# Regrouping the tail, a packed head and casting transfers in an attention and feed-forward kernel

## The chip, the cores and the metric

The kernel runs on one core of a Trainium2 chip. The metric is device time of one launch in microseconds, lower is better. Five engines work side by side and are tied by semaphores: PE (TensorE, the matmuls; its weight loads stand apart as PEld), DVE (VectorE), ACT (ScalarE), POOL (GpSimd) and SP (SyncE, which mostly issues transfers). Transfers between HBM and the core's SBUF are carried out by 16 DMA engines.

## The reference

Linear attention with decay over 4 batches, 8 heads, 768 tokens and head dimension 64, then a bilinear feed-forward with 512 inputs and 1536 inner columns. All inputs and the output are float32. The attention goes block by block and carries a 64 x 64 state for each batch and head:

```python
for b in range(nb):
    qb, kb, vb = (q[:, :, sl], k[:, :, sl], v[:, :, sl])
    intra = einsum('bhic,bhjc->bhij', qb, kb) * Dmask
    intra = einsum('bhij,bhjd->bhid', intra, vb)
    inter = einsum('bhid,bhde->bhie', qb * lam_pow, kv_state)
    out[:, :, sl] = intra + inter
    kv_state = lam_block * kv_state + einsum('bhsd,bhse->bhde', kb * rev_pow, vb)
x = out.transpose(0, 2, 1, 3).reshape(3072, 512)
return ((x @ w_a) * (x @ w_b)) @ w_out
```

## The kernel before

**Units and groups.** The 3072 tokens are 24 units of 128 tokens, six to a batch, each with all 8 heads. GROUPS cuts the units into groups, g0 to g7, of 4, 1, 2, 4, 4, 4, 4 and 1 units. A group's attention is written transposed into a tile xT (four slices s of 128 features by up to 512 tokens), and then its feed-forward runs while the attention of the next group's units is woven in.

**Attention of a unit.** q and k are multiplied by powers of lambda and cast to bf16 (scale, L401, called by make_ks and make_qs), v is cast (make_vb, L418 and L420). q and k are transposed, by PE (piece_T) for units 4 to 6 and by a transposing transfer of SP (in prep_k) from unit 7 on. scores (kq, L457) are 8 matmuls, two to a head pair; mask (L480) multiplies them by the triangle lotri; intra and inter (o_mm, L497) build o_ps, which evac_o copies to xT (L520). kv_update and kv_copy keep the state.

**The head.** Units 0 to 3 are the first group, and nothing can be hidden under a feed-forward yet. Their q and k are loaded with 4 tokens to a partition, so that rows are 1 KB long (x4), scaled (scale4, L877), transposed (transpose4, L886), and put back in natural order of tokens by the copies of unpack (L897). natural_k transposes k once more. v is loaded in natural order. scores4 (L922) and the functions above do the rest; warm issues idle matmuls.

**Weights.** w_a and w_b come in six chunks of 256 columns each, w_out in six of 256 rows, all as f32 by SP's queue into staging tiles (load_w, tile wst), and are cast to bf16 by DVE, ACT or POOL (cast_w, L240 to L254) while g0 runs. A list, pending, holds the order of all loads; pump issues the next as soon as a staging slot is free or, for q, k and v, the unit is no more than LOOKAHEAD ahead.

**Feed-forward.** Plain groups (g0, g1, g2, g7) take for each of the 12 blocks f of 128 inner columns four matmuls for a (a_ps) and four for b (b_ps, both L596); ACT copies a (L605), DVE multiplies (L623), and the product is multiplied by w_out (op, L643). Groups 3 to 6 (Z_GROUPS) make a and b by seven half-size products in place of eight (ffn_z, tiles U, V, W, L730): the halves of xT are added and subtracted first (x_sums, L705 to L707), so are the quarters of the weights (weight_sum, L267 to L275), and ACT and DVE put the products together in a tile oab (L736, L767 to L769), whose halves DVE multiplies into ab (L738). Groups 4 to 6 (ZO_GROUPS) make the multiplication by w_out by seven products too, in 14 halves H (out_half, L852), which are woven into the next group's feed-forward; they need sums of ab (ab_sum, SM in the plan) and of w_out (out_sum, WO). The last group is one plain unit, between whose matmuls the halves H of g6 stand; its output leaves in three pieces, of 256, 128 and 128 columns.

**Order.** PLAN is a table written by hand: for each group, at which slot of the feed-forward which piece (T, S, V, O, P, C, H, ...) is issued. Each engine works through its own instructions in the order in which they are issued. The tables VB_ENG, KV_ENG, SUM_ENG, XS_ENG and the like choose the engine of a piece.

Of the kernel before, what the change touches and what calls it, by code (L numbers as in the profile page):

```python
# [22 lines left out]
def _bc(ap, dims):  # L23
# [8 lines left out]
LOOKAHEAD = {9: 2, 10: 1}  # L32
DMA_T = range(7, 24)
KEEP_GROUPS = 2
PACK = 4

PLAN = {
# [38 lines left out]
}  # L81
Z_GROUPS = (3, 4, 5, 6)
ZO_GROUPS = (4, 5, 6)
FIN_AT = 5
N_LATE = 3
EV_ENG = {(u, b): "act" for u in range(24) for b in range(2)}
MASK_ACT = dict(enumerate([0] * 7 +
                        [1] +
                        [0] * 3 +
                        [1] * 2 +  # L90
                        [0] * 4 +
                        [1] * 3 +
                        [0] +
                        [1] +
                        [0] * 2))
KV_ENG = dict(enumerate(["dve"] * 10 + ["act"] * 2 + ["dve"] + ["act"] * 11))
VB_ENG = dict(enumerate(["pool"] * 7 +
                        ["dve"] * 3 +
                        ["pool"] * 5 +
                        ["dve"] * 2 +  # L100
                        ["act"] +
                        ["pool"] +
                        ["dve"] +
                        ["pool"] +
                        ["act"] * 3))
SUM_ENG = {(3, 0): 'dve', (3, 1): 'dve', (3, 2): 'pool', (3, 3): 'dve', (3, 4): 'pool', (3, 5): 'pool', (3, 6): 'dve', (3, 7): 'dve', (4, 0): 'dve', (4, 1): 'pool', (4, 2): 'pool', (4, 3): 'pool', (4, 4): 'dve', (4, 5): 'pool', (4, 6): 'pool', (4, 7): 'pool', (5, 0): 'dve', (5, 1): 'dve', (5, 2): 'pool', (5, 3): 'pool', (5, 4): 'dve', (5, 5): 'pool', (5, 6): 'pool', (5, 7): 'dve', (6, 0): 'pool', (6, 1): 'dve', (6, 2): 'pool', (6, 3): 'dve', (6, 4): 'dve', (6, 5): 'pool', (6, 6): 'dve', (6, 7): 'dve'}
XS_ENG = {(3, 0): 'dve', (3, 1): 'dve', (3, 2): 'dve', (4, 0): 'dve', (4, 1): 'dve', (4, 2): 'dve', (5, 0): 'dve', (5, 1): 'pool', (5, 2): 'pool', (6, 0): 'pool', (6, 1): 'pool', (6, 2): 'pool'}
WS_ENG = {0: 'dve', 1: 'dve', 2: 'dve', 3: 'dve', 4: 'dve', 5: 'dve', 6: 'dve', 7: 'pool'}
WO_ENG = {0: 'dve', 1: 'dve', 2: 'pool', 3: 'dve', 4: 'dve'}
CO_ENG = {0: 'pool', 1: 'pool', 2: 'pool', 3: 'dve', 4: 'dve', 5: 'dve'}  # L110
# [3 lines left out]
def kernel(  # L114
# [40 lines left out]
    raw_pool = ctx.enter_context(tc.tile_pool(name="raw", bufs=1))  # L155
# [16 lines left out]
    def z_bank(name, i):  # L172
        return ps_pool.tile([128, 2, 256], F32, name=name, tag=f"ps{i}")
# [5 lines left out]
    raw = {}  # L179

    def load_x(w, u):
        b, nb = divmod(u, NB)
        if w == "v" and u == GROUPS[0] - 1:
            t = o_pool.tile([128, H, D], F32, name="vf", tag="osb")
        else:
            t = ld_pool.tile([128, H, D], F32, name=w + "f", tag=w + "f")
        nc.sync.dma_start(out=t, in_={"q": qr, "k": kr, "v": vr}[w][b, nb])
        raw[u, w] = t
# [7 lines left out]
    staged = {}  # L196
    HN, NP = d_model // 2, FC // 2

    def sum_tile(shape, dt, name, tag):
        return sum_pool.tile(shape, dt, name=name, tag=tag)  # L200

    ab_stage = ab_pool.tile([128, 3, 1024], F32, name="wst", tag="ab")
    slots = [lambda: oab_pool.tile([128, 1024], F32, name="wst", tag="oab")] * 2
    slots += [lambda i=i: ab_stage[:, i] for i in range(3)]
    slots += [lambda t=t: sum_tile([128, 1024], F32, "wst", t) for t in ("zab", "wy0", "wy1")]
    once = lambda: xT_pool.tile([128, 1024], F32, name="wst", tag="xT")
    slots.insert(0, once)
# [8 lines left out]
    def load_w(kind, c):  # L216
        slot = slots.pop(0)
        t = slot()
        if kind == "o":
            t = t.rearrange("p (k n) -> p k n", k=2)  # L220
            nc.sync.dma_start(out=t, in_=wo_r[:, 2 * c:2 * c + 2, :])
        else:
            w = W_CHUNKS[c]
            t = t[:, :KS * w].rearrange("p (k n) -> p k n", k=KS)
            r = wa_r if kind == "a" else wb_r
            if c in W_HALVES:
                t = t.rearrange("p k n -> p (k n)").rearrange("p (k n) -> p k n", k=2)
            nc.sync.dma_start(out=t, in_=w_part(r, c))
        staged[kind, c] = t, slot

    def cast_w(kind, c, eng):
        t, slot = staged.pop((kind, c))
        if slot is not once:
            slots.append(slot)
        if kind == "o":
            dst = wo_sb[:, 2 * c:2 * c + 2, :]
        else:
            dst = w_part(wa_sb if kind == "a" else wb_sb, c)
        if eng == "act":
            nc.scalar.copy(dst, t)  # L240
        elif eng == "pool":
            nc.gpsimd.tensor_copy(dst, t)
# [50 lines left out]
    for cs in W_STEPS:  # L293
        pending += [("a", c) for c in cs] + [("b", c) for c in cs]
# [784 lines left out]
```

## Time and profile before

| | |
|---|---|
| median of 3 runs | 227.97 us (226.08 to 229.54) |
| the profiled execution | span 224.7 us; no time of its own is given beside the span |
| granted TensorE clock | 1.00 in all stages |
| PE, DVE, ACT, POOL busy | 214.6, 164.8, 123.2, 101.1 us |
| matmuls | 2235 |
| transfers by queue | all by SP but the lambdas and the last output piece (ACT's queue) |
| moved | HBM read 28.32 MB, written 6.29 MB |
| first matmul of g0, g1, ... g7 | 18.16, 53.19, 64.33, 84.74, 118.67, 143.10, 175.23, 203.74 us |
| last matmul ends | 221.74 us |

A row of the profile's groups reads: line, engine, operation, output <- inputs, shapes, count | busy us, mean ns of one | idle time of the engine just before them, and what ended most of it. Lines are those of the kernel before. "PEclk" is the share of full clock that TensorE was granted.

### The profile page before, as it was taken

The numbers are of one execution on the slowest core, as the hardware profiler recorded it, in microseconds if no ns is written. First come the engines' busy times: TensorE is split into PE (matmuls) and PEld (weight loads), VectorE is DVE, ScalarE is ACT, GpSimd is POOL, SyncE is SP. The second block draws the span as 40 slices with busy tenths as digits, with TensorE's granted clock in tenths as the row PEclk, the third lists the DMA queues.
The fourth block names the chain that finished last, engine by engine and source line by source line (L and its number), as shares of the span: only waits on it lengthen the run. The fifth ranks groups of instructions, "written<-read, shape, count | busy, mean of one in ns | idle before, by whom it ended". The sixth has DMA issues, their size and how long they took to land.

```text
span 224.7 us, 5609 instructions
## 1 busy us (share of the span) xinstructions
PE 214.6 (96%) x2235; PEld 158.8 (71%) x2235; DVE 164.8 (73%) x269; ACT 123.2 (55%) x251; POOL 101.1 (45%) x95
## 2 busy tenths in 40 slices
PE   7699999989989999999999999899999999999994
PEld 2375444437768757887547878688888888887994
DVE  1895673599699659989878999968686765777440
ACT  3586446017544247775366988776536665533322
POOL 6061004256895075541459359786417722052000
PEclk9999999999999999999999999999999999999999
DMA  4999999998999999999999999652021100112042
GB/s 137 316 231 356 356 384 346 276 217 192 229 198 218 219 180 240 204 253 247 175 240 243 243 206 202 138 98 48 2 88 55 50 1 4 47 48 95 0 143 93
DMA packets 99081, 39.42 MB, mean 175 GB/s; under 512 B 85488, under 2 KB 95088, under 8 KB 99056
## 3 DMA queue, kind: packets, MB, share of 16 engines
q1 hardware_dynamic: 98768, 39.00, 78.0%
q8 instruction: 17, 0.28, 0.5%
q10 hardware_dynamic: 288, 0.07, 0.1%
q14 instruction: 8, 0.07, 0.1%
HBM read 28.32 MB, written 6.29 MB: 154 GB/s over the span
## 4 chain that ended last, share of the span: by engine, by line
PE 80%; DVE 6%; DMA 6%; ACT 3%; issue 2%; SPq 1%; ACTq 0%; DVEq 0%
PE U L730 17%; PE op L852 12%; PE b_ps L596 9%; PE op L643 8%; PE V L730 8%; PE a_ps L596 8%; PE op L792 5%; PE W L730 4%; DMA wst<-in_moe_w_b_dram 4%; PE o_ps L497 3%; DMA k<-in_k_dram 3%; PE kq L457 2%; PE kvd L527 1%; SPq L350 1%; DVE m L480 1%
## 5 line engine op out<-in xcount | busy, mean ns | idle before, releaser
L811 ACT COPY u<-U 128x512 f32<-128x512 f32 x48 | 28.4, 591 | 16.9 <-PE U L730 16.6
L401 POOL TENSOR_TENSOR qk<-kf,lp_k 128x512 bf16<-128x512 f32 x18 | 19.8, 1099 | 34.6 <-DMA kf<-in_k_dram 23.1
L623 DVE TENSOR_TENSOR ab<-a_sb,b_ps 128x128 bf16<-128x128 bf16 (+2 forms) x48 | 19.2, 417 | 14.0 <-ACT a_sb L605 11.1
L480 DVE TENSOR_TENSOR m<-kq,lotri 128x512 bf16<-128x512 f32 x40 | 25.7, 684 | 3.8 <-PE kq L457 3.6
L596 PE MATMUL a_ps<-xT,wa_sb 128*128 128x128 bf16 (+2 forms) x200 | 27.8, 268 | 0.6 <-ACT xT L520 0.5
L596 PE MATMUL b_ps<-xT,wb_sb 128*128 128x128 bf16 (+2 forms) x192 | 27.5, 272 | 0.7 <-ACT oab L736 0.5
L738 DVE TENSOR_TENSOR ab<-oab 128x1024 bf16<-128x1024 bf16 x24 | 18.4, 767 | 10.5 <-ACT oab L736 10.5
L401 POOL TENSOR_TENSOR qk<-qf,lp_q 128x512 bf16<-128x512 f32 x20 | 25.2, 1259 | 1.2 <-DMA qf<-in_q_dram 1.2
L605 ACT CAST a_sb<-a_ps 128x128 bf16<-128x128 f32 (+2 forms) x48 | 17.1, 375 | 14.4 <-PE a_ps L596 14.3
L643 PE MATMUL op<-wo_sb,ab 128*128 128x512 bf16 (+2 forms) x120 | 22.8, 337 | 0.2 <-DVE wo_sb L254 0.2
L596 PEld LDWEIGHTS <-wa_sb 128*128 128x128 bf16 x200 | 16.6, 98 | 6.6 <-issue 0.7
L596 PEld LDWEIGHTS <-wb_sb 128*128 128x128 bf16 x192 | 15.7, 98 | 7.3 <-DVE wb_sb L251 0.7
L730 PEld LDWEIGHTS <-wz_a 128*128 128x128 bf16 x192 | 18.2, 98 | 3.6 <-issue 0.7
L730 PEld LDWEIGHTS <-wz_b 128*128 128x128 bf16 x192 | 18.7, 98 | 2.2
L730 PE MATMUL U<-xT,wz_a 128*128 128x256 bf16 x96 | 18.3, 272 | 0.0
L730 PE MATMUL U<-xT,wz_b 128*128 128x256 bf16 x96 | 18.3, 272 | 0.0
L520 ACT CAST xT<-o_ps 128x512 bf16<-128x512 f32 (+1 forms) x24 | 12.2, 556 | 10.7 <-PE o_ps L497 10.5
L420 POOL CAST vb<-vf 128x512 bf16<-128x512 f32 x14 | 10.9, 778 | 13.9 <-DMA vf<-in_v_dram 13.9
L769 DVE TENSOR_TENSOR oab<-U,u 128x512 bf16<-128x512 f32 x24 | 16.4, 682 | 0.4 <-PE U L730 0.4
L730 PEld LDWEIGHTS <-wa_sb 128*128 128x128 bf16 x144 | 13.4, 97 | 4.5 <-issue 1.7
L643 PEld LDWEIGHTS <-ab 128*128 128x128 bf16 x120 | 10.1, 98 | 8.6 <-issue 0.3
L736 ACT CAST oab<-U 128x512 bf16<-128x512 f32 x24 | 14.2, 591 | 3.6 <-PE U L730 3.5
(126 smaller groups left out, 453.8 us busy)
## 6 DMA issues: line engine op xcount, KB each, us to landing
vf<-in_v_dram SPq DMA_DIRECT2D x24, 256.0 KB, 4.8
qf<-in_q_dram SPq DMA_DIRECT2D x20, 256.0 KB, 4.6
kf<-in_k_dram SPq DMA_DIRECT2D x20, 256.0 KB, 4.6
out_dram<-o_sb SPq DMA_DIRECT2D x18, 256.0 KB, 2.5
wst<-in_moe_w_a_dram SPq DMA_DIRECT2D x6, 512.0 KB, 8.5
wst<-in_moe_w_b_dram SPq DMA_DIRECT2D x6, 512.0 KB, 9.0
wst<-in_moe_w_out_dram SPq DMA_DIRECT2D x6, 512.0 KB, 10.6
out_dram<-o_kept SPq DMA_DIRECT2D x5, 256.0 KB, 4.4
```

The source lines that it names most:

```text
L401: eng_of(eng).tensor_mul(dst.rearrange("p (c b) d -> p b c d", b=2), x[:].rearrange("p (b c) d -> p b c d", b=2), lp.rearrange("p (b c) o ...
L480: nc.vector.tensor_mul(m, kq[i], lotri_bc)
L596: nc.tensor.matmul(ps[:, lo:hi], lhsT=w_sb[:, s, f * 128:(f + 1) * 128], rhs=xT[:, s, lo:hi], start=(s == 0), stop=(s == KS - 1), skip_gro ...
L605: nc.scalar.copy(a_sb[:, :gt], ps[:, :gt])
L623: nc.vector.tensor_mul(ab[:, f, :gt], a_sb[:, :gt], ps[:, :gt])
L643: nc.tensor.matmul(op[:, lo:hi], lhsT=ab[:, f, t * 128:(t + 1) * 128], rhs=wo_sb[:, f, lo:hi], start=(f == 0), stop=(f == FC - 1))
L730: nc.tensor.matmul(ps[:, k, :], lhsT=wt[:, s, n * 128:(n + 1) * 128], rhs=rhs[i][:, s, :], start=(fresh and k == 0 and s == 0), stop=True, ...
L736: nc.scalar.copy(oab[:, 0], U)
L738: nc.vector.tensor_mul(ab[:].rearrange("p (h i) (t c) -> p h i t c", h=2, t=2)[:, :, n], o5[:, :, :, 0, :], o5[:, :, :, 1, :])
L769: nc.vector.tensor_sub(oab[:, 1], U, v1)
L811: nc.scalar.copy(t, ps)
L852: nc.tensor.matmul(ps[:, t, :], lhsT=lhs[p][:, n, t * 128:(t + 1) * 128], rhs=rhs[:, n, :], start=fresh, stop=True, skip_group_check=True)
```

## The change

- **Groups.** 4, 1, 3, 4, 4, 4, 4. g2 has three units and is a Z group with halves of 192 columns and a plain output; g3 to g6 make the output by seven products as well; the plain unit at the end is gone, and the last group issues its own 14 halves H after its products. The last output piece is one store of 256 KB after an ACT copy.
- **Weights and v.** Chunks of weights and v of units 4 to 23 are loaded by transfers that GpSimd issues and that cast f32 to bf16 on the way, straight into the place of use: 36 transfers on POOL's queue (10 of w_a and w_b, 6 of w_out, 20 of v). Chunks 0 and 1 of w_a come as f32 by SP (load_first), and are cast in pieces by ACT and POOL (A4). Staging tiles, pending and pump are gone; each load has a slot in PLAN (LQ, LK, LV, LW).
- **Head.** v of units 0 to 3 is packed as q and k are, and everything stays in packed order until the copies to xT (evac4). A unit's tokens are 32 partitions, so the matmuls of scores, intra and state work on 32-row tiles: scores4 128 matmuls, intra4 128, states4 96, inter4 48. natural_k and unpack are gone; the masks use a triangle tri4 in packed order, which POOL makes with five instructions. The load, scale, transpose and other steps of the head are pieces of PLAN too (group -1).
- **Pieces.** What was one piece is several now: scaling of k and q (PK, PQ), transposes (TR), scores (S), masks (M), state update and copy (V, K), output matmuls and copies (O, E), the products' multiplication (MU, `times`), the three sums of xT (X). VAR chooses a piece's engine: 17 of the 30 MU go to POOL, the transposes of units 4, 5 and 7 to PE, and those of unit 6 and 8 to 23 to transposing transfers. A plain group packs four blocks f of one unit into one bank (ffn_plain), so that three copies and multiplications take the place of twelve.
- **Gate.** Ahead of the loads of q and k of units 4, 5 and 6, DVE writes one element of the destination (GATED).

PE issues 2505 matmuls with 529,920 columns in place of 2235 with 508,160.

```diff
-GROUPS = (4, 1, 2, 4, 4, 4, 4, 1)
+GROUPS = (4, 1, 3, 4, 4, 4, 4)
+Z_GROUPS = (2, 3, 4, 5, 6)
+ZO_GROUPS = (3, 4, 5, 6)
...
+GATED = (4, 5, 6)
 PACK = 4
+N_VB = 8
...
+        (29, 'LQ', 7), (29, 'LW', ('o', 2)), (32, 'LK', 7), (38, 'LW', ('o', 4)), (38, 'PQ', 5),
+        (41, 'TR', 5), (42, 'LV', 5), (43, 'PQ', 6), (43, 'TR', 6), (43, 'LW', ('o', 5)), (43, 'WO', 1),
+        (43, 'PK', 7), (43, 'V', 4), (43, 'LK', 8), (43, 'PQ', 7), (44, 'W', 0), (44, 'O', (4,)),
+        (44, 'E', ((4,), 1)), (44, 'E', ((4,), 0)), (44, 'LV', 6), (44, 'LK', 11), (46, 'K', 4),
...
+        if w == "v" and u >= n0:
+            t = prep_pool.tile([128, H, D], BF16, name="vb", tag="vb", bufs=N_VB)
+            nc.gpsimd.dma_start(out=t, in_=vr[b, nb])
+        else:
...
+            if u in GATED:
+                nc.vector.memset(t[0:1, 0, 0:1], 0.0)
+            nc.sync.dma_start(out=t, in_={"q": qr, "k": kr, "v": vr}[w][b, nb])
...
+    def load_w(x):
+        kind, c = x
         if kind == "o":
...
+            nc.gpsimd.dma_start(out=wo_sb[:, 2 * c:2 * c + 2, :], in_=wo_r[:, 2 * c:2 * c + 2, :])
+        else:
+            w, r = (wa_sb, wa_r) if kind == "a" else (wb_sb, wb_r)
+            nc.gpsimd.dma_start(out=w_part(w, c), in_=w_part(r, c))
...
+    def load_first(c):
+        first[c] = (xT_pool if c == 0 else oab_pool).tile([128, KS, 256], F32, name="w0",
+                                                          tag="oab" if c else "xT")
+        nc.sync.dma_start(out=first[c], in_=w_part(wa_r, c))
...
+    def times(x):
+        g, n = x
+        hw = outs[g]["hw"]
+        o5 = oabs[x][:].rearrange("p (h t) k c -> p h t k c", h=2)
+        dve_pool("MU", x).tensor_mul(
...
+            o5[:, :, :, 0, :], o5[:, :, :, 1, :])
...
-    def natural_k(us, hps, at):
...
+    def scores4(c):
...
         for r in range(PACK):
...
+            for b in range(2):
+                p = slice(64 * b, 64 * b + 64)
+                for u in range(n0):
+                    x = slice(32 * u, 32 * u + 32)
+                    nc.tensor.matmul(kq[b][x, r], lhsT=xT4[p, c, 1, r, x], rhs=xT4[p, c, 0, :, x],
+                                     start=True, stop=True, skip_group_check=True)
...
+    def cast_first(x):
+        c, k0, k1, lo, hi = x
+        dst, src = wa_sb[:, k0:k1, 256 * c + lo:256 * c + hi], first[c][:, k0:k1, lo:hi]
+        i = var("A4", x)
+        if i == 2:
+            nc.scalar.copy(dst, src)
+        else:
+            (nc.gpsimd if i else nc.vector).tensor_copy(dst, src)
```

More of the change, by code (lines that the diff above doesn't have):

```diff
@@ L31 @@
 W_HALVES = (4, 5)
-LOOKAHEAD = {9: 2, 10: 1}
-DMA_T = range(7, 24)
-KEEP_GROUPS = 2
+GATED = (4, 5, 6)
 PACK = 4
+N_VB = 8
+KEEP = 5
 PLAN = {
[38 rows of a table removed]
-}
[L82 to L95, printed above, removed]
@@ new lines @@
+T4_WARM = ((2, 192), (2, 192), (2, 192), (2, 192))
+VAR = {('A4', (0, 0, 3, 0, 128)): 2,
+  ('A4', (0, 0, 4, 128, 256)): 1,
+  ('A4', (0, 3, 4, 0, 128)): 1,
+  ('A4', (1, 0, 4, 0, 256)): 1,
+  ('C4', 1): 2,
+  ('C4', 2): 2,
+  ('C4', 3): 2,
+  ('E', ((4,), 0)): 1,
+  ('E', ((7,), 0)): 1,
+  ('E', ((10, 11), 0)): 1,
+  ('E', ((20, 21), 0)): 1,
+  ('E', ((22, 23), 0)): 1,
+  ('E4', 2): 1,
+  ('E4', 3): 1,
+  ('K', 3): 1,
+  ('K', 4): 1,
+  ('K', 7): 1,
+  ('K', 8): 1,
+  ('K', 10): 1,
+  ('K', 16): 1,
+  ('K', 18): 1,
+  ('K', 20): 1,
+  ('K4', (0, 0, 4)): 1,
+  ('M', 4): 2,
+  ('M', 8): 2,
+  ('M', 10): 1,
+  ('M', 16): 1,
+  ('M', 17): 2,
+  ('M', 20): 1,
+  ('M', 22): 1,
+  ('M4', (2, 0)): 1,
+  ('M4', (3, 1)): 1,
+  ('MU', (2, 1)): 1,
+  ('MU', (2, 2)): 1,
+  ('MU', (2, 3)): 1,
+  ('MU', (2, 5)): 1,
+  ('MU', (3, 1)): 1,
+  ('MU', (3, 4)): 1,
+  ('MU', (4, 1)): 1,
+  ('MU', (4, 2)): 1,
+  ('MU', (4, 4)): 1,
+  ('MU', (4, 5)): 1,
+  ('MU', (5, 0)): 1,
+  ('MU', (5, 3)): 1,
+  ('MU', (5, 4)): 1,
+  ('MU', (5, 5)): 1,
+  ('MU', (6, 0)): 1,
+  ('MU', (6, 1)): 1,
+  ('MU', (6, 3)): 1,
+  ('P4', ('k', 3)): 1,
+  ('P4', ('q', 3)): 1,
+  ('PK', 4): 1,
+  ('PK', 5): 1,
+  ('PK', 6): 1,
+  ('PK', 7): 1,
+  ('PK', 9): 1,
+  ('PK', 11): 1,
+  ('PK', 13): 1,
+  ('PK', 15): 1,
+  ('PK', 16): 1,
+  ('PK', 18): 1,
+  ('PK', 22): 1,
+  ('PK', 23): 1,
+  ('PQ', 4): 1,
+  ('PQ', 6): 1,
+  ('PQ', 7): 1,
+  ('PQ', 10): 1,
+  ('PQ', 11): 1,
+  ('PQ', 14): 1,
+  ('PQ', 15): 1,
+  ('PQ', 19): 1,
+  ('PQ', 22): 1,
+  ('SM', (3, 0)): 1,
+  ('SM', (3, 1)): 1,
+  ('SM', (3, 4)): 1,
+  ('SM', (3, 5)): 1,
+  ('SM', (3, 6)): 1,
+  ('SM', (3, 7)): 1,
+  ('SM', (4, 1)): 1,
+  ('SM', (4, 4)): 1,
+  ('SM', (4, 5)): 1,
+  ('SM', (5, 1)): 1,
+  ('SM', (5, 5)): 1,
+  ('SM', (5, 6)): 1,
+  ('SM', (5, 7)): 1,
+  ('SM', (6, 0)): 1,
+  ('SM', (6, 4)): 1,
+  ('TR', 6): 1,
+  ('TR', 8): 1,
+  ('TR', 9): 1,
+  ('TR', 10): 1,
+  ('TR', 11): 1,
+  ('TR', 12): 1,
+  ('TR', 13): 1,
+  ('TR', 14): 1,
+  ('TR', 15): 1,
+  ('TR', 16): 1,
+  ('TR', 17): 1,
+  ('TR', 18): 1,
+  ('TR', 19): 1,
+  ('TR', 20): 1,
+  ('TR', 21): 1,
+  ('TR', 22): 1,
+  ('TR', 23): 1,
+  ('WO', 1): 1,
+  ('WO', 4): 1,
+  ('WS', 6): 1,
+  ('X', (2, 0)): 1,
+  ('X', (2, 2)): 1,
+  ('X', (5, 1)): 1,
+  ('X', (6, 0)): 1,
+  ('X', (6, 1)): 1}
@@ L536, in kv_update @@
         if u % NB == NB - 1:
+            return
+        if u == n0 - 1:
+            ps = kv_bank()
+            for c in range(HP):
+                for r in range(PACK):
+                    nc.tensor.matmul(ps[:, c, :, :], lhsT=xs4["k"][:, r, 2 * c * D:2 * (c + 1) * D],
+                                     rhs=vb4[c][:, :, r, :], start=(c == 0 and r == 0), stop=True,
+                                     skip_group_check=True)
             return
@@ new lines, in ffn, with ffn_plain @@
+        ops = [ps_bank("op", [128, d_model], F32, hold=True) for _ in range(n)]
+        for c in range(FC // 2):
+            for t in range(n):
+                out_mms(ops[t], ab, t, range(2 * c, 2 * c + 2))
+                if c == FC // 2 - 1:
+                    store(u0 + t, ops[t])
+                hook(slot)
+                slot += 1
+        bank["held"].clear()
+    def ffn_plain(u0, n, xT, hook):
+        gt = n * BLK
+        ab = ab_pool.tile([128, FC, 512], BF16, name="ab", tag="ab")
+        nf = 512 // gt
+        slot = 0
+        for c in range(0, FC, nf):
+            pss = []
+            for w_sb, name in ((wa_sb, "a_ps"), (wb_sb, "b_ps")):
+                ps = ps_bank(name, [128, nf, gt], F32, ffn=True)
+                for f in range(nf):
+                    for s in range(KS):
+                        nc.tensor.matmul(ps[:, f, :], lhsT=w_sb[:, s, (c + f) * 128:(c + f + 1) * 128],
+                                         rhs=xT[:, s, :gt], start=(s == 0 and f == 0), stop=True,
+                                         skip_group_check=True)
+                    if f == nf // 2 - 1:
+                        hook(slot)
+                        slot += 1
+                if name == "a_ps":
+                    a_sb = xz_pool.tile([128, nf, gt], BF16, name="a_sb", tag="xz")
+                    nc.scalar.copy(a_sb, ps)
+                else:
+                    nc.vector.tensor_mul(ab[:, c:c + nf, :gt], a_sb, ps)
+                hook(slot)
+                slot += 1
+        plain_out(u0, n, ab, hook, slot)
@@ new lines, in plain_out @@
+    def plain_out(u0, n, ab, hook, slot, last=(FC - 1,)):
+        ops = [ps_bank("op", [128, d_model], F32, ffn=True) for _ in range(n)]
+        first = [f for f in range(FC) if f not in last]
+        for t in range(n):
+            out_mms(ops[t], ab, t, first, first[0], last[-1])
+            hook(slot)
+            slot += 1
+        for t in range(n):
+            out_mms(ops[t], ab, t, last, first[0], last[-1])
+            store(u0 + t, ops[t])
+            hook(slot)
+            slot += 1
@@ L984 @@
-    cast_w("a", 0, "first")
-    evac_o((2, 3), 0)
-    evac_o((2, 3), 1, eng="dve")
-    natural_k((3,), (0, 1, 2, 3), 3)
-    bank["held"].clear()
-    cast_w("a", 1, "dve")
-    cast_w("b", 0, "cols")
-    used["u"] = n0
-    if N_LATE:
-        late_stage = sum_pool.tile([128, 3, 1024], F32, name="wst", tag="wz_a")
-        slots += [lambda i=i: late_stage[:, i] for i in range(N_LATE)]
-    pump()
+    xT4 = scr[0][:, 4:12, :].rearrange("p (c w) (r x) -> p c w r x", c=HP, r=PACK)
+    vb4, m4, kq4 = {}, {}, {}
@@ new lines, with first4, o4_banks, intra4 @@
+    o4, d4 = [], []
+    new4 = set()
+    def first4(*x):
+        if x in new4:
+            return False
+        new4.add(x)
+        return True
+    def o4_banks(u):
+        while len(o4) <= u:
+            i = len(o4)
+            if i == 2:
+                o4.append(kvps_pool.tile([128, 2 * 2, PACK, 32], F32, name="o4", tag="kvd"))
+            else:
+                o4.append(ps_bank("o4", [128, 2 * 2, PACK, 32], F32, at=(5, 6, None, 0)[i]))
+        return o4[u]
+    def intra4(cs):
+        for b in range(2):
+            for r in range(PACK):
+                for c in cs:
+                    for u in range(n0):
+                        x = slice(32 * u, 32 * u + 32)
+                        h = slice(64 * (c % 2), 64 * (c % 2) + 64)
+                        nc.tensor.matmul(o4_banks(u)[h, 2 * b + c // 2], lhsT=vb4[c][x, b, r, :],
+                                         rhs=m4[c][x, b, r], start=first4("o", u, c % 2), stop=True,
+                                         skip_group_check=True)
@@ new lines, in states4 @@
+    def states4(x):
+        cs, ws = x
+        for w in ws:
+            if len(d4) <= w:
+                d4.append(ps_bank(f"d{w}", [128, HP, D], F32, at=1 + w))
+        for c in cs:
+            for r in range(PACK):
+                for b in range(2):
+                    for w in ws:
+                        x = slice(32 * w, 32 * w + 32)
+                        s = (2 * c + b) * D
+                        nc.tensor.matmul(d4[w][64 * b:64 * b + 64, c], lhsT=xs4["k"][x, r, s:s + D],
+                                         rhs=vb4[c][x, b, r, :], start=first4("d", w, b), stop=True,
+                                         skip_group_check=True)
```

760 lines of the change are left out of this document (294 added, 466 removed), and 133 rows, old and new, of the table PLAN.

## The prediction

> **What bounds the kernel now.** I read the page's busy shares first, then a table of windows by stage, then the chain that ended last, then the groups and the DMA issues that the change touches.
>
> ```profile
> span 224.7 us, 5609 instructions
> PE 214.6 (96%) x2235; PEld 158.8 (71%) x2235; DVE 164.8 (73%) x269; ACT 123.2 (55%) x251; POOL 101.1 (45%) x95
> DMA  4999999998999999999999999652021100112042
> ```
> TensorE (PE) is busy 96% of the span; the DMA engines are full for the first two thirds (some 26 slices of 5.6 us), then nearly free.
>
> The windows cut the span at the first feed-forward matmul of each group. Columns: window, length, busy time of PE, weight load, DVE, ACT, POOL, granted clock, DMA share, GB/s.
> ```profile
> 0.00:18.16 18.16, 14.62 (x184) 8.57 (x184) 11.89 (x21) 10.43 (x19) 7.63 (x24) 1.00 0.86 237
> 18.16:53.19 35.03, 33.90 (x192) 16.13 (x193) 23.08 (x34) 14.91 (x25) 8.26 (x9) 1.00 1.05 310
> 64.33:84.74 20.41, 20.30 (x240) 14.92 (x240) 15.39 (x28) 8.61 (x21) 11.06 (x12) 1.00 1.19 206
> 84.74:118.67 33.93, 33.60 (x330) 23.61 (x328) 30.17 (x47) 20.36 (x40) 15.38 (x15) 1.00 1.27 229
> 203.74:224.70 20.96, 17.50 (x218) 16.11 (x215) 8.09 (x21) 6.55 (x20) 1.64 (x1) 1.00 0.23 76
> ```
> In each stage PE nearly fills the window, and the clock is 1.00, so the time is PE's column count plus its few waits. The head (18.16 us, DMA share 0.86) is the exception: it waits for loads. In the chain (start, length, what) the steps off PE are few; these are two of them, with PE steps that give prices:
> ```profile
> 32.67 3.45 PE a_ps L596 x16
> 45.29 0.60 DVE qk L401
> 45.89 0.61 DVE wo_sb L254
> 53.36 0.22 PE a_ps L596 x4
> 78.08 0.55 PE kq L457 x16
> 146.32 0.92 PE o_ps L497 x32
> 153.13 0.87 PE U L730 x8
> ```
> Prices: 512 columns 3.45/16 = 0.216 us, 256 columns 0.87/8 = 0.109, 128 columns 0.22/4 = 0.055, kq 0.034, o_ps 0.029. PE's wait at 45-46 us is a weight cast (wo_sb, L254) behind another DVE piece.
>
> **The sum of before.** Feed-forward: a plain group of 4 is 144 x 0.216 = 31.1; a plain unit 96 x 0.055 + 12 x 0.216 = 7.9; the plain pair 96 x 0.109 + 24 x 0.216 = 15.6; a Z group with plain out 168 x 0.109 + 48 x 0.216 = 28.7; a group with all in seven products 252 x 0.109 = 27.5. In order 31.1 + 7.9 + 15.6 + 28.7 + 3 x 27.5 + 7.9 = 173.7. Attention of units 4 to 23 by its counts (160 kq, 296 o_ps, 68 of state and transpose at 0.055, 40 short): 18.3. Head 18.2, end after the last matmul 2.9. What is left of 224.7 is 11.6 of waits and switches of form. I make all sums against this span; the median of the runs (227.97) is 3.3 above it, and I add that at the end.
>
> **The change part by part.**
>
> *Groups.* After: g0 31.1, g1 7.9, g2 (3 units, seven products on 192 columns) 168 x 0.082 + 36 x 0.216 = 21.5, g3 to g6 27.5 each: 170.5, so -3.2. The 192-column price is an estimate on the line between 0.055 and 0.109; at worst it costs like 256, +4.5; at best like 128, -4.5. The attention counts of units 4 to 23 are unchanged.
>
> *Head.* Everything of units 0 to 3 stays packed: 16 second transposes (natural_k) and their ACT copies go, scores4, intra4 and states4 become 352 small matmuls on 32 rows. PE had 3.5 us free in the head, so these don't set its end; the loads do. In before the first q pieces land at 5 and the last k at 11; then now four v pieces of 1 KB rows follow in place of v in short rows (the one that POOL needs at about 12.8), then two f32 weight chunks by SP to about 17. Then ACT and POOL pieces (A4) cast chunk 0, 0.3 to 0.6 us each, and the first matmul comes at 17.2 to 18.5. But POOL's own queue sets a second date: after its set-up (8.6), two scalings (10.8) and the cast of v piece 0 (13.4) it issues six casting transfers (LW) and only then casts its 128x128 (0.4 us): 13.4 + 6d + 0.4, d being what one issue holds POOL. The trace has no transfer issued by POOL. Nearest below: SP's issue of a transfer, 0.46 (L350). Nearest above: POOL's longest instruction, 3.09:
> ```profile
> L275 POOL TENSOR_TENSOR wz_b<-wb_sb x1: 3088/3088/3088, 61.7 to 61.7; 128x1536 bf16<-128x1536 bf16 x1
> L275 DVE TENSOR_TENSOR wz_a<-wa_sb x1: 1792/1792/1792, 65.0 to 65.0; 128x1536 bf16<-128x1536 bf16 x1
> ```
> Issuing is what SP does in 0.46, so I take a value near that end, 0.7: POOL's date is 18.0 and I take a head of 18.3 (+0.1). Bounds: 17.2 (d at 0.46) and 32.3 (d at 3.09).
>
> [...]
>
> *Weight and v casts.* On DVE, ACT and POOL 30-odd cast instructions go:
> ```profile
> vf<-in_v_dram SPq DMA_DIRECT2D x24, 256.0 KB, 4.8
> wst<-in_moe_w_b_dram SPq DMA_DIRECT2D x6, 512.0 KB, 9.0
> L420 POOL CAST vb<-vf 128x512 bf16<-128x512 f32 x14 | 10.9, 778 | 13.9 <-DMA vf<-in_v_dram 13.9
> L738 DVE TENSOR_TENSOR ab<-oab 128x1024 bf16<-128x1024 bf16 x24 | 18.4, 767 | 10.5 <-ACT oab L736 10.5
> ```
> Gone from the path: PE's waits for casts in g0 (0.36 at 21.6, 0.90 and 0.36 at 45-46): -1.6. Instead 36 issues stand in POOL's queue (36 x 0.7 = 25 us of it), and WO(1) waits there for the transfer of o(5) issued just before it (landing about 57); v of units 6 and 7 is issued behind it and needed in g1 from 61.5. With 4.8 us to landing that is level: 0, up to +1.
>
> *Freed DVE time.* By my count of instructions by stage, DVE falls from 165 to 149 us and POOL rises from 101 to 116 plus the issues, since 17 of 30 multiplies of products (MU; L738 above, always DVE before) go to POOL. On POOL one should cost 2.13, as z_sub of the same size does there (L705). Waits of PE for DVE in before: 0.5 at 85.5 (z_add), 0.98 at 142.0 (oab). Finer pieces placed by slot should take most of them: -0.9 of 1.5; no less than 0.
>
> *No g7.* One switch of groups goes with its wait (0.66 at 203.9 for oab, ACT): -0.7. The end: ACT copy of 512 columns 0.6 and one 256 KB store 2.5, with some issue 3.4, against 2.9: +0.5.
>
> *DMA.* Before, a load of q, k or v lands every 1.17 us while the engines are full, a weight chunk every 1.5, a transpose every 1.15. By the order of issue after, the transposes of units 11 and 10 have 29 loads and three transposes ahead of them and would end near 85; g2 needs them at 79 and 81. Stalls of 0 to 6.7 us. The casting transfers write half the bytes; if their time goes by bytes read and written, each is a quarter shorter and the lateness is gone. I take +1.0.
>
> **The sum.** Head 18.3 + feed-forward 170.5 + attention 18.3 + waits (11.6 - 1.6 - 0.9 - 0.7 + 1.0 = 9.4) + end 3.4 = 219.9, 4.8 below the span of before. With 3.3: **223.2 us**. A measurement of this kernel can tell about 2% from no change, so the bounds are 223.4 and 232.5; the forecast lies on the first.
>
> **The rivals.**
>
> A, clearly faster: POOL issues at SP's price, transfers are not late, finer pieces take 3 us more of the waits that I leave standing. Head 17.4 + 170.5 + 18.3 + waits 6.4 + 3.4 = 216.0, so 219.3. For it: DVE idles 10.5 us for oab alone and 16 us of its work go. Against: PE's 96% leaves little to find.
>
> B, slower: GpSimd's queue. [...] Place: the casts A4 behind six LW, and v6, v7 behind WO(1). Each microsecond of d above 0.7 is 6 us of head: at d = 1.4 the gain is used up (+4.2), at 2.1 (+8.4, and +1 in g1) it is slower by 2%, at 2.3 the head ends at 27.6 and the time is 223.2 + 9.3 + 1 = 233.5. For it: POOL's instructions in before are all slow (0.78 for a cast that DVE does in 0.42). Against: an issue is no pass over data.
>
> C, the DMA engines in g2: T11 and T10 at 85, +5.7 over my sum, 228.9, within 2%. For it: the share of 1.19 to 1.27 there before. Against: half the written bytes.
>
> D, DVE and POOL in each other's way. L275 on DVE took 1.79 wholly beside POOL, and L271 of the same size 0.95 alone; multiplies (L738) beside POOL took 0.89, alone 0.69. In g3 DVE has 21.0 us of work by my count against PE's 20.4; 20% more on it is 4 us there: 227.2. [...]
>
> **How the numbers follow.** Forecast 0.36 (faster 0.19, same 0.16, slower 0.01), A 0.23 (faster), B 0.26 (slower 0.22, same 0.04), C 0.10 (same 0.08, slower 0.02), D 0.05 (same 0.04, slower 0.01). Together faster 0.42, same 0.32, slower 0.26. The range runs from A with one more microsecond off each of head, waits and 192-column price (about 216) to B at d = 2.5 (235): 216 to 235. The forecast's own range is 220 to 227.
>
> **What would show it.** Right: first a_ps at 17.2 to 19; 168 U, V, W products of g2 at 0.082; no PE wait for wa_sb, wb_sb or wo_sb; last matmul 3.4 before the end. Wrong: POOL busy or held 2 us at each transfer with a_ps beyond 20 (B); PE waiting for qkT at 79 to 85 (C); DVE's multiplies above 0.9 and PE waiting for oab in g3 to g5 (D). The forecast falls if the span is under 216 or over 224.

## The result, and the profile after

The changed kernel takes 242.8 us (median of 6 runs, 241.9 to 244.4) where the kernel before took 226.8 in the same session: a ratio of 1.072, with an interval of 1.066 to 1.078. It is slower by 16 us; the prediction said 223.2.

The busy times of the page, and the windows by stage (window, length, PE, weight load, DVE, ACT, POOL, granted clock, DMA share, GB/s). The stages are the head, g0, g1, g2, g3, g4, g5, and g6 with the end.
```profile
span 241.6 us, 6101 instructions
PE 219.6 (91%) x2498; PEld 165.8 (69%) x2505; DVE 172.3 (71%) x264; ACT 118.9 (49%) x227; POOL 140.7 (58%) x123
PEclk9769599999999999999999799999999999999999
DMA  4999999909969999999999097089416012100314
```
```profile
0.00:30.39 30.39, 19.83 (x470) 13.43 (x470) 13.16 (x24) 12.88 (x20) 21.50 (x42) 0.78 1.08 230
30.39:64.95 34.56, 34.24 (x211) 17.08 (x212) 20.59 (x32) 12.26 (x21) 13.82 (x12) 1.00 1.02 147
64.95:75.61 10.66, 10.61 (x171) 8.26 (x169) 8.25 (x12) 4.78 (x9) 4.50 (x5) 1.00 1.00 152
75.61:106.92 31.31, 28.31 (x331) 20.88 (x332) 29.98 (x45) 16.28 (x36) 18.16 (x17) 1.00 1.23 171
106.92:134.82 27.90, 24.70 (x279) 19.79 (x276) 24.06 (x34) 16.95 (x34) 19.62 (x15) 0.96 1.24 190
134.82:166.66 31.84, 30.80 (x341) 24.98 (x340) 25.84 (x41) 18.56 (x36) 24.27 (x15) 0.99 0.68 111
166.66:197.67 31.01, 31.01 (x352) 26.39 (x350) 24.30 (x42) 19.04 (x38) 19.84 (x12) 1.00 0.27 50
197.67:241.62 43.95, 40.09 (x362) 34.99 (x359) 26.14 (x40) 18.20 (x34) 19.03 (x11) 1.00 0.22 73
```
The head lasts 30.4 us in place of 18.2 and its mean clock is 0.78: 12.2 of the 16.9 us of span are lost before the first feed-forward matmul. From there to the last matmul, which ends at 237.85, it takes 207.5 in place of 203.6, though the feed-forward has 3.2 us less of matmuls. By the prices of the prediction and the matmuls recorded in each window, the time of a stage exceeds PE's work by some 5.8 us in g2, 5.8 in g3 and 3.3 in g4, where no stage of before exceeded it by more than 2.5; g0, g1, g5 and g6 stay within 2. The end, after the last matmul, takes 3.8.

The chain of the head (start, length, what) shows where:
```profile
17.45 0.54 PE o L1063 x38
18.00 0.54 issue
18.88 0.83 PE d L1078 x95
19.88 5.13 issue
25.01 1.29 PE o L1063 x51
26.30 2.70 PE o L1099 x48
29.00 1.46 PE kvd L636 x16
30.46 1.18 PE a_ps L690 x10
```
"issue" is time in which PE waited for nothing that the profile shows. Ahead of it stand 95 matmuls in 0.83 us (L1078 is states4, L1063 intra4, L1099 inter4): the matmuls on 32-row tiles run beside each other (each of L1078 takes 0.18 to 0.21 us), so PE goes through 190 instructions, weight loads counted, in less than a microsecond. The packet records hold a queue of the kind "instruction" (q8 of the page: 17 transfers of 16 KB before, 19 after). From 150 us on, after, one starts for every 240 to 268 instructions that PE has issued, 253 in the mean. I take them for PE's code and a block for 256 instructions, an estimate from that count; they then start 176 to 206 instructions into a block. Taking 180 as the trigger, a reckoning that is good to some 20 instructions:

```
               PE at its trigger   fetch starts   wait   PE instructions issued by then
before, 1st         13.7 us            18.5        4.8        376
before, 2nd         24.1               27.5        3.4        468
after, 1st          13.6               16.0        2.5        300
after, 2nd          17.7               22.7        5.0        705 (no more came until 25.0)
before, 13th       164.2              164.4        0.2       3256
```
In these early stretches, with the DMA engines full, a fetch waits 2.5 to 5 us by this reckoning. A full share alone does not make it so: from 45 to 130 us, where the share is still 0.8 to 1.5, the waits reckoned in this way are 0 to 2.7 us in both kernels; what sets the difference stays open. In the kernel before, PE issued some 20 instructions a microsecond in the head (376 by 18.5) and did not run out by this reckoning; after, it issued its 705th at 19.7 and the next at 25.0, 1.5 us after the fetch that started at 22.7 had landed. I read that as a wait for code; experiments 1 to 3 test it. The clock records give half speed at 9.4 to 16.3 us, at 23.1 to 29.9, behind that wait, and once more at 132.3 to 135.7 in g3 and g4. The stretches last 6.8, 6.8 and 3.4 us. In the 3.4 us ahead of them PE was busy for 44%, 5% and 50%; what sets them off is not shown.

In g2 to g4, the waits of PE that are longest are for DVE (oab: 0.8 us at 79.8, 0.5 at 92.5, 0.7 at 127.2, 1.9 at 130.8) and for transposing transfers (1.4 at 95.2, 0.9 at 141.9), 6.2 us together. In g2 and then g3 (line waited for: us in total, times, longest):
```profile
PE kq L553 <- DMA qkT<-qk: 1.4, 1, 1.4
PE U L859 <- DVE oab L899: 0.8, 1, 0.8
```
```profile
PE op L968 <- DVE oab L884: 1.9, 1, 1.9
```
What made DVE late, in order of time:
```profile
77.47 1.05 POOL L506 TENSOR_TENSOR qk<-kf,lp_k 128x512 bf16<-128x512 f32 x1
77.52 2.56 DVE L506 TENSOR_TENSOR qk<-kf,lp_k 128x512 bf16<-128x512 f32 x1
78.47 1.04 POOL L506 TENSOR_TENSOR qk<-qf,lp_q 128x512 bf16<-128x512 f32 x1
80.00 0.55 DVE L899 TENSOR_TENSOR oab<-U,u 128x384 bf16<-128x384 f32 x1
123.07 1.03 POOL L506 TENSOR_TENSOR qk<-kf,lp_k 128x512 bf16<-128x512 f32 x1 [1.99 <-DMA kf<-in_k_dram]
123.20 1.45 DVE L830 TENSOR_TENSOR ab<-oab 128x1024 bf16<-128x1024 bf16 x1
124.06 0.94 POOL L344 DMA_DIRECT2D vb<-in_v_dram  x1
129.18 2.12 POOL L830 TENSOR_TENSOR ab<-oab 128x1024 bf16<-128x1024 bf16 x1 [2.51 <-ACT oab L865]
129.55 2.30 DVE L830 TENSOR_TENSOR ab<-oab 128x1024 bf16<-128x1024 bf16 x1
```
DVE's instructions of L506 and L830 have two SBUF inputs and take 0.68 to 0.69 us alone (128x512 and 128x1024). Each of the three here ends 0.5 to 0.6 after a computing instruction of POOL does, so I read the rest of its time as standing until POOL was done. Those of L899 (128x512), which have an input in PSUM, take the same 0.68 to 0.69 beside POOL's computing (20 of them) as alone (4). At 77.52 DVE stood through two of POOL's instructions. That is the exception: of the 15 DVE instructions that took over 0.08 us more than the shortest of their form, nearly all others were let in after one, and POOL's next one then stood (1.49 us in place of 1.04 at 143.96) or, where it was the issue of a transfer, ran beside DVE (124.06). The kernel before shows the same wait, and there a cast with one SBUF input has it too (L420, 2.21 at 62.9, the shortest 0.42): by the excess over the shortest of each form, DVE's instructions lost 11.0 us there and 15.2 after, noise counted in both.

### The profile page after: what moved, and what is told of

It reads as the page before. It is cut to its first block, busy times and chain, and to the rows that moved or that the text cites. A ratio compares the mean times of both kernels' runs of the same rounds, so it can differ in the third digit from the quotient of the medians.

```text
span 241.6 us, 6101 instructions
## 1 busy us (share of the span) xinstructions
PE 219.6 (91%) x2498; PEld 165.8 (69%) x2505; DVE 172.3 (71%) x264; ACT 118.9 (49%) x227; POOL 140.7 (58%) x123
## 4 chain that ended last, share of the span: by engine, by line
PE 69%; DVE 9%; DMA 7%; issue 5%; ACT 3%; POOL 3%; SPq 1%; DVEq 0%; ACTq 0%; POOLq 0%
PE U L859 15%; PE op L968 15%; PE V L859 8%; PE op L735 5%; PE a_ps L690 4%; PE b_ps L690 4%; PE W L859 4%; DMA kf<-in_k_dram 3%; DMA out_dram<-o_kept 2%; PE o_ps L592 2%; DMA q<-in_q_dram 2%; PE kq L553 2%; ACT scratch L1004 2%; DVE qk L506 2%; PE t L1003 1%
## 5 line engine op out<-in xcount | busy, mean ns | idle before, releaser
L921 ACT COPY u<-U 128x512 f32<-128x512 f32 (+1 forms) x60 | 34.2, 571 | 39.8 <-PE U L859 37.1
L830 POOL TENSOR_TENSOR ab<-oab 128x1024 bf16<-128x1024 bf16 (+1 forms) x17 | 35.3, 2078 | 23.5 <-ACT oab L865 20.9
L859 PE MATMUL U<-xT,wz_a 128*128 128x256 bf16 (+1 forms) x120 | 22.5, 270 | 0.2 <-ACT u L921 0.2
L859 PE MATMUL U<-xT,wz_b 128*128 128x256 bf16 (+1 forms) x120 | 22.5, 269 | 0.0
L968 PEld LDWEIGHTS <-ab 128*128 128x128 bf16 x192 | 18.7, 99 | 4.6 <-issue 1.9
L735 PE MATMUL op<-wo_sb,ab 128*128 128x512 bf16 x92 | 21.5, 379 | 0.2
L899 DVE TENSOR_TENSOR oab<-U,u 128x512 bf16<-128x512 f32 (+1 forms) x30 | 19.7, 655 | 2.8 <-PE U L859 2.6
L968 PE MATMUL op<-wy,ab 128*128 128x256 bf16 x144 | 19.3, 278 | 1.9 <-DVE oab L884 1.9
L859 PEld LDWEIGHTS <-wa_sb 128*128 128x128 bf16 x180 | 16.9, 98 | 5.8 <-issue 2.9
L506 POOL TENSOR_TENSOR qk<-kf,lp_k 128x512 bf16<-128x512 f32 x8 | 8.7, 1082 | 19.4 <-DMA kf<-in_k_dram 14.3
L344 POOL DMA_DIRECT2D vb<-in_v_dram x20 | 18.4, 922 | 1.4 <-PE kvd L636 1.4
L921 ACT COPY u<-V 128x512 f32<-128x512 f32 (+1 forms) x30 | 17.2, 573 | 3.2 <-PE V L859 1.7
L506 DVE TENSOR_TENSOR qk<-kf,lp_k 128x512 bf16<-128x512 f32 x12 | 14.2, 1184 | 3.4 <-DMA kf<-in_k_dram 3.4
L506 POOL TENSOR_TENSOR qk<-qf,lp_q 128x512 bf16<-128x512 f32 x11 | 11.9, 1085 | 7.6 <-DVE ab L717 5.0
L735 PEld LDWEIGHTS <-ab 128*128 128x128 bf16 x96 | 9.1, 98 | 10.1
## 6 DMA issues: line engine op xcount, KB each, us to landing
wo_sb<-in_moe_w_out_dram POOLq DMA_DIRECT2D x6, 256.0 KB, 11.2
```

The source lines that it names most:

```text
L344: nc.gpsimd.dma_start(out=t, in_=vr[b, nb])
L506: eng.tensor_mul(dst.rearrange("p (c b) d -> p b c d", b=2), x[:].rearrange("p (b c) d -> p b c d", b=2), lp.rearrange("p (b c) o -> p b c ...
L735: nc.tensor.matmul(op, lhsT=ab[:, f, t * 128:(t + 1) * 128], rhs=wo_sb[:, f, :], start=(f == f0), stop=(f == f1))
L830: dve_pool("MU", x).tensor_mul(outs[g]["ab"][:].rearrange("p (h i) x -> p h i x", h=2)[:, :, n, :2 * hw] .rearrange("p h (t c) -> p h t c" ...
L859: nc.tensor.matmul(ps[:, k, :], lhsT=wt[:, s, n * 128:(n + 1) * 128], rhs=rhs(i)[:, s, :], start=(fresh and k == 0 and s == 0), stop=True, ...
L899: nc.vector.tensor_sub(oab[:, 1], U, v1)
```

## The experiments

Times are spans of the profiled execution (after: 241.6; before: 224.7) and medians. "Body" is the time from the first feed-forward matmul to the end of the last matmul (after: 207.5; before: 203.6).

**1. Two bursts of small matmuls in the kernel before.**
```diff
+    def burst(n):
+        ps = ps_bank("idle", [128, 8, 64], F32)
+        for k in range(n):
+            c = k % 2
+            nc.tensor.matmul(ps[64 * c:64 * c + 64, k % 8, :16], lhsT=wa_sb[0:32, 0, 0:64],
+                             rhs=wa_sb[0:32, 1, 0:16], start=True, stop=True, ...)
...
+            if (g, slot) in ((0, 3), (6, 12)):
+                burst(256)
```


> The kernel before, with two bursts of 256 small matmuls (32 rows, 16 columns, output unused) added: one in g0 where the DMA engines are full, one in g6 where they are nearly idle. Each burst is 512 PE instructions (weight load and matmul), two blocks of 16 KB of code. Theory (code fetch): a block is fetched by the same DMA engines when the one before is some two thirds done; in the full phase it waits 2.5 to 5 us behind data, so PE stalls with 'issue' for 4 to 8 us in the g0 burst, and for no more than 1 to 2 us a block in g6. Rival (small row tiles are slow by themselves, or a switch of tile form costs): both bursts take the same time, within 1 us.

Waits of PE around the burst in g0, then around that in g6 (line waited for: us in total, times, longest):
```profile
PE a_ps L596 <- issue: 3.3, 1, 3.3
PE idle L1001 <- issue: 2.2, 1, 2.2
```
```profile
PE idle L1001 <- issue: 0.8, 1, 0.8
```
Span 249.0, one run. 5.5 us of "issue" where the DMA engines are full (share 1.07 in that window), 0.8 where they are nearly idle (0.03). The fetches concerned waited 6.3 and 6.3 us in g0, 0.6 and 2.1 in g6. The burst with its waits took 11.2 and 6.1. The same instructions, so neither the tiles nor a switch of form makes the wait. Half clock came with the burst in both places (0.68 and 0.71 in the windows). In g6 it began at 214.4, while the small matmuls ran without a gap (211.9 to 215.8): no wait is needed for it, and these matmuls did not hold the clock. The span grew by 24.3 us, 7 more than the two bursts took; where the rest comes from stays open.

**2. Casting transfers of weights behind the head's small matmuls (changed kernel).**
```diff
+        (-1, 'K4', (0, 0, 4)), (-1, 'G', 1), (-1, 'LW', ('b', 1)), (-1, 'LW', ('b', 0)),
+        (-1, 'LW', ('a', 2)), (-1, 'LW', ('b', 2)), (-1, 'LW', ('a', 3)), (-1, 'LW', ('b', 3)),
+        (-1, 'LW', ('a', 4)), (-1, 'LK', 5), (-1, 'LK', 4),
...
+    def gate(c):
+        nc.vector.memset(wb_sb[0:1, 0, 256 * c:256 * c + 1], 0.0)
```


> The changed kernel, with the casting weight transfers and the k loads of units 4 and 5 moved behind the head's small matmuls: a one-element write by DVE after the state copies holds the first of them back, and the casts of the first weight chunk go ahead of them on POOL. Theory (PE's code fetch waits behind the transfers): PE's 5.3 us wait at 19.7 shrinks below 1.5, the half clock after it goes, and g0 starts near 23.5 to 25 in place of 30.4; later stages lose up to 2 us to later weights. Rival (the head is long by its own work, PE waits for masks and copies): g0 starts no earlier than 29.

PE's waits from 15 to 30 us, for the changed kernel and for this run:
```profile
PE o L1063 <- issue: 5.7, 2, 5.1
```
```profile
PE o L1067 <- issue: 2.0, 2, 1.7
```
The second fetch started at 19.1 in place of 22.7, the long wait fell from 5.1 to 1.7, and g0 started at 27.1: 3.3 earlier, the way that the theory has it, though less than it said. The clock was half from 10.1 to 27.2. Body 207.4; median 240.7, ratio to before 1.066 (1.059 to 1.072).

**3. Three quarters of the packed intra and state matmuls left out.** All transfers stay.
```diff
     def intra4(cs):
         for b in range(2):
-            for r in range(PACK):
+            for r in range(1):
...
     def states4(x):
...
-            for r in range(PACK):
+            for r in range(1):
```


> The changed kernel, with intra4 and states4 done for one of the four token places in a partition (32 and 24 matmuls in place of 128 and 96): three quarters of the intra part and of the states of units 0 to 3 are left out, and 336 PE instructions (1.3 blocks of code); all transfers stay. Theory (code fetch behind full DMA queues): PE reaches the end of the head before its 705th instruction, so the wait of 5.3 us at 19.7 is gone or below 1.5, and g0 starts 6 to 8 us earlier than 30.4, at 22.5 to 24.5, of which the matmuls left out are some 1.5. Rival (the head waits for masks, copies and casts in any case): g0 starts at 27 or later.

PE's waits from 15 to 30 us:
```profile
PE d L1078 <- DVE m L1025: 0.8, 1, 0.8
PE o L1063 <- DVE m L1028: 0.6, 1, 0.6
PE kq L1015 <- ACT scratch L1004: 0.2, 1, 0.2
```
No "issue" is left among them. The second fetch started at 22.3, as late as ever, but PE had issued only 570 instructions by then and did not run dry. g0 started at 24.1: 6.2 us earlier. The span is 229.7 (median 232.0). The half clock lasted from 10.3 to 24.0 all the same.

**4. Idle matmuls to hold the clock,** with the late transfers of 2, and with the shorter code of 3.
```diff
-HEAD_WARM = (13,)
-T4_WARM = ((2, 192), (2, 192), (2, 192), (2, 192))
+HEAD_WARM = (20,)
+T4_WARM = ((9, 256), (9, 256), (9, 256), (9, 256))
```


> The run with late weight transfers, and idle matmuls added in the head where PE waited for q, k and copies: 20 of 512 columns in place of 13 at its start, 9 of 256 after each of the four packed transposes in place of 2 of 192. Theory (the head runs at half clock from 10 us because PE is too little busy before): the granted clock stays 1.00 to the end of the head and g0 starts 3 to 5 us earlier, at 22 to 24. Rival (small row tiles don't count as work for the clock, or the head waits for copies anyway): half clock remains, or g0 moves by less than 1 us.

> The run with a quarter of the small matmuls, and the idle matmuls of the run with late transfers (20 of 512 columns at the start, 9 of 256 after each packed transpose). Theory (with the fetch wait gone, the half clock from 10 to 24 us is what keeps the head at 24.1): clock 1.00 through the head and g0 starts at 22 or before. Rival (loads, masks and copies keep it there): g0 starts within 0.7 of 24.1, whatever the clock.

With 2, the clock was full until 19.8, and g0 started at 27.4 (27.1 without): nothing gained (median 243.9), and half clock came back just as the wait for code began (19.3 to 21.5). With 3, the clock was full until 20.2, then half, and g0 started at 23.3 in place of 24.1. So the first half-clock stretch costs 0 to 0.9 us: PE waits there for copies anyway. The clock was a smaller cause than I held. The tail of that head is PE's own chain after the last loads, most of it at half clock:
```profile
18.33 0.30 PE d L1078 x24
18.65 0.42 DVE st L1089
19.10 0.44 DVE st L1089
19.58 2.07 PE o L1099 x44
21.66 1.82 PE kvd L636 x16
23.48 1.53 PE a_ps L690 x13
```
In the kernel before the first a_ps stood at 18.2, where here the states are just being made.

**5. POOL's multiplications cut to an eighth of their columns.**
```diff
+        w = hw // 8 if var("MU", x) else hw
...
+        dve_pool("MU", x).tensor_mul(dst[:, :, :, :w], o5[:, :, :, 0, :w], o5[:, :, :, 1, :w])
+        if w < hw:
+            nc.gpsimd.memset(dst[:, :, :, w:], 0.0)
```


> The changed kernel; each of POOL's 17 multiplications of products is done on an eighth of its columns and the rest of the output is set to zero (a write that reads no SBUF), so seven eighths of these products are left out of the result. POOL's order and DVE's work stay. Theory (lock: a POOL instruction that reads SBUF holds up DVE's instructions with two SBUF inputs, and POOL itself is late): DVE's scalings and multiplications return towards 0.69, PE's waits for oab of 2.1 at 130.6 and 0.9 at 126.9 and 79.6 go, and the span is 4 to 7 us shorter. Rival (DVE's and PE's order of pieces and late transposes set these waits): under 1.5 us shorter.

Span 237.1, median 238.8, body 203.6; PE's 1.9 us wait at 130.8 fell to 0.3, but the waits of 0.8 at 79 and 0.6 at 126 stayed: there it is POOL's scalings and a sum of ab that DVE stood behind (two of 1.0 us, and one of 1.65).

**6. Most of v not loaded,** units 8 to 23 use v of unit 7.
```diff
+        if w == "v" and u >= 8:
+            raw[u, w] = raw[7, w]
+            return
```


> The changed kernel, with v loaded for units up to 7 only; units 8 to 23 use v of unit 7, so 16 casting transfers of some 2.1 us of all DMA engines each, and 16 issues of 0.9 us on POOL, are left out. Theory (g2 to g4 lose mostly to the lock, little to DMA): PE's waits for qkT (1.57 at 94.9, 1.05 at 141.6) go, some 3 us less in all. Rival (the DMA engines' lateness behind the k loads sets the stages): g2 and g3 become 6 us or more shorter together.

g2 became 27.9 (31.3) and lost its wait for qkT; g3 became 29.3 (27.9), with 3.6 us of new waits of PE for ACT's copies u: their tiles held kept outputs of g0 and g1, whose stores landed at 113.4 and 117.1. Span 239.8, median 241.3, body 205.1. Neither theory holds as it stands: g2 gained 3.4 us, g3 lost 1.4 by another wait, and PE's wait for qkT in g4 stayed (1.2 at 140.0).

**7. Cuts 3, 5 and 6 together.**

> The run before, with two earlier cuts joined: POOL's multiplications on an eighth of their columns, and v loaded up to unit 7 only (the results leave out what those runs left out). If code fetch, lock and late transfers are separate causes, the gains add: head 6 to 8, lock 3.8, transfers 2 to 3, so a span of 227 to 230 against 241.6. If they cover one another or another cause stands behind them (copies kept in the snapshot tiles until their stores, the order of pieces), the span stays above 231.

Span 231.7, median 232.9, above that of cut 3 alone (229.7). The gains do not add. And a caution comes out: the changed kernel, cut 3 and cut 3 with idle matmuls have the same body to the letter, started at 30.4, 24.1 and 23.3, and it took 207.5, 201.7 and 205.3. So a difference of under 6 us between bodies cannot be put down to an edit, and experiments 5 and 6 do not measure the shares of the lock (DVE standing behind POOL) and of the transfers.

**8. The engine split of before.** First 13 of POOL's 17 multiplications given to DVE; then DVE's 18 scalings from unit 6 on to POOL as well; then the scalings alone. Each takes entries out of VAR.

> The changed kernel, with 13 of the 17 multiplications of products that POOL does given to DVE, at the same places. Theory (DVE's SBUF operations stand behind POOL's long ones): the 13 cost DVE 0.69 each, 9 us, but its held-up scalings and multiplications lose most of their 14 us; the waits for oab in g2 to g4 (0.94, 0.65, 0.89, 2.1) mostly go: 2 to 5 us less than the changed kernel. Rival (DVE simply has too much work there): 2 to 5 us more. Rival (late transposes by DMA set g2 to g4): within 1 us.

> As the run before, and the 18 scalings of q and k of units 6 on that DVE does given to POOL, which does those of all units from 6 on as in the kernel before. Theory (lock): DVE's scalings, mean 1.18 us, leave it, so DVE loses 20 us of work and waits against the changed kernel; PE's waits in g2 to g4 go down to those of before: 4 to 7 us less than the changed kernel, with the head unchanged at 30. Rival (late transposes): POOL's scalings are later, transposes too, and nothing is gained.

> The changed kernel, with the 18 scalings of q and k of units 6 on that DVE does given to POOL; the multiplications of products stay where they are. Theory (DVE's instructions with two SBUF inputs stand behind POOL's chain of instructions, and the scalings are the ones that stand longest, 7.5 us in all): DVE loses 20 us, PE's waits for oab shrink, 2 to 4 us less than the changed kernel. Rival (POOL is then the bound: 20 us more on it between 43 and 185 us, scalings and so transposes later): 2 us or more slower than the changed kernel.

Spans 257.2, 258.8 and 250.5, times of the profiled runs 258.9, 260.6 and 252.2: all three much slower, against my theory. The multiplications, at the same places in DVE's order, stood ahead of what PE needed (waits of PE of 2.4 us for z_sub at 110.8, 2.3 for masks at 114.7), and beside POOL's other work they were held up still (6.5 us over their time alone). The scalings on POOL stood ahead of the last weight transfers in its queue, and waited for k:
```profile
PE op L717 <- DMA wo_sb<-in_moe_w_out_dram: 5.4, 1, 5.4
```
The placement is tied to the split: these runs say nothing of what the split is worth with its pieces placed for it.

**9. One part alone: v by casting transfers in the kernel before.**
```diff
+        if w == "v" and u >= GROUPS[0]:
+            t = prep_pool.tile([128, H, D], BF16, name="vb", tag="vb", bufs=6)
+            nc.gpsimd.dma_start(out=t, in_=vr[b, nb])
+            raw[u, w] = t
+            return
```


> The kernel before, with one part of the change alone: v of units 4 to 23 by casting transfers of POOL, six buffers, and no cast instructions for it. Theory (a casting transfer occupies the DMA engines longer, 2.06 us in place of 1.5 for one v, 11 us in all while they are full, and its issue holds POOL 0.92 us, about as long as its cast took): later loads, 0 to 3 us slower than before (about 226 to 229). Rival (the casting transfers are what costs the middle of the changed kernel): 5 us or more slower. Rival (they help, as casts leave three engines): 1 us or more faster.

236.1 us, ratio 1.046 (1.034 to 1.058); span 232.2, 7.5 over before. That is the rival's 5 us or more: the part alone costs, in a kernel whose other pieces were not placed anew for it; that it is also what costs the middle of the changed kernel is not shown. The trace shows two ways. By the means of the packet records one v occupies each of the 16 engines 2.06 us as a casting transfer (1024 packets of 32 ns) and 1.5 us without the cast (23.5 ns). And once DVE stood through three of POOL's instructions, an issue among them:
```profile
119.13 1.04 POOL L406 TENSOR_TENSOR qk<-qf,lp_q 128x512 bf16<-128x512 f32 x1
119.33 6.54 DVE L295 TENSOR_TENSOR wy<-wo_sb 128x1536 bf16<-128x1536 bf16 x2
120.11 0.94 POOL L185 DMA_DIRECT2D vb<-in_v_dram  x1
121.08 3.10 POOL L295 TENSOR_TENSOR wy<-wo_sb 128x1536 bf16<-128x1536 bf16 x1
```
The first of the two DVE instructions took 5.68 us, 0.95 alone, and ended 0.8 after the third of POOL's; PE then waited 2.7 for z_sub. Here the issue did not let DVE in, where at 124.06 in the changed kernel it did; what decides is open. The two ways are not separated here.

## Why the prediction was wrong

**The head: the step that failed first.** I wrote that 352 small matmuls "don't set its end; the loads do", because PE had 3.5 us free, and added 0.1 us. The head became 12.2 us longer. The step has no term for the code that their instructions use up. PE's wait for code is 5.1 of the 12.2; with three quarters of the intra and state matmuls left out the wait was gone and 6.2 were won (cut 3), some 1.7 of them the matmuls themselves (L1063 and L1078 keep PE busy for 3.4 us after and for 1.7 in the cut). The rest, 5.1 to 5.9 us, is left with the wait for code out of the way and all transfers in place: a longer chain after the last load, with 44 to 48 inter matmuls, 16 for the state, half clock in part of it, and copies to xT that take 1.30 in packed order against 0.59 before (L520). What of this sets the remainder stays open.

**d, the price of an issue on POOL,** was about right: I took 0.7, and it measured 0.70 to 0.96 for weights and 0.88 to 0.95 for v. POOL's first cast of chunk 0 ended at 17.9, for which I had said 18.0. So rival B fell in the place I gave it; that its head of 27.6 is nearer to the 30.4 measured than mine is luck, since the reason is another. B's sums took 2.1 to 2.5 us for d, which no run shows: the longest issue of POOL measured in the changed kernel is 0.96. With the scalings alone on POOL (8), its queue did make a weight late, by 5.4.

**Waits: 9.4 predicted, 18.7 measured** (207.5 less 170.5 and 18.3). The casts' waits in g0 went, as forecast, but g0 became only 0.5 shorter. The part "Freed DVE time" failed: finer pieces did not take the waits for DVE, and DVE was not freed. I counted 149 us of its work, down from 165, and it was busy 172. Of that 14 is standing behind POOL: 7.5 in seven scalings, 3.2 in four multiplications (L830: 0.86 to 2.30, 0.69 alone). But some 10 us of such standing were in the 165 as well, so it is the smaller part of the miss. The larger part is work: with the standing taken off, DVE had some 154 us before and 157 after, where I had it fall by 16. One reason on view is that VAR gives DVE 21 of the 40 scalings of q and k of units 4 to 23 (21.8 us with their standing), where DVE did 2 before and POOL 38; where else the count was short stays open. Rival D priced the standing at 4 us in g3 and gave it a chance of 0.05; g3 exceeds PE's work by some 4 us more than in before (5.8 against 1.6), but how much of that is the standing is not shown. POOL's 141 us were as forecast (116 and 25).

**Transfers.** "Half the written bytes" should have made them shorter; a casting v took 1.37 times as long on the engines (2.06 us against 1.5, experiment 9). The transposes of units 11 and 10 landed at 88.7 and 96.5, where I had said 85 (rival C), and PE waited 1.4 for one. How the loss in g2 to g4 (waits of 18.7 in all in place of 9.4) divides between lock, DVE's own work, transfers and the half clock at 132.3 stays open, for the reason given under 7.

**Right:** the 192-column price (0.66 for 8, so 0.082), the feed-forward sum with its 3.2 us, and the end (3.8 against 3.4). With the head of before and the body of cut 3 the sum would be 18.2 + 201.7 + 3.8 = 223.7, 1 us under before. That is a sum and no run; no kernel tried here beat the one before.

## What to carry to other kernels

Count PE's instructions in a stretch, not only its columns: small tiles that run beside each other used up code here faster than it arrived in the head, where the DMA engines were full (190 instructions in 0.83 us, then a wait of 5.1), and the profile shows it only as "issue". An instruction moved to POOL can cost DVE too, where DVE has two SBUF inputs: 15 of them were held here, one for 2.56 us in place of 0.68. Count too what moves the other way: 19 scalings went from POOL to DVE, the engine that was to be freed. And before crediting an edit with a few microseconds, look how far the same code, started at another time, differs from itself.

## What I had not expected of the hardware

By the reckoning above, a code fetch of 16 KB waited 2.5 to 6.3 us in the early stretches, with the DMA engines full, 0 to 2.7 later with them still busy, and under 1 when they were idle, with one of 2.1 in a burst. Small matmuls that ran without a gap from 211.9 to 215.8 did not hold the clock (the burst in g6: half from 214.4). Of the 15 DVE instructions held by POOL in the changed kernel, nearly all were let in after one POOL instruction, but one stood through two (2.56 us), and in experiment 9 one stood through three (5.68 us), one of them a transfer's issue.
